# A windowed attention and gated convolution kernel: batch 0 in two token halves, rows of h turned by engine copies, loads not paced, new target times

## The chip, the cores and the metric

The kernel runs on one core of one Trainium2 chip. The metric is the device time of one execution in microseconds, the median of several runs. Before the change it is 241.77 us, the median of three runs (241.15, 241.77, 247.62).

A core has five engines that run side by side: TensorE (PE; its weight loads are shown apart, as PEld) for matmuls, VectorE (DVE), ScalarE (ACT) and GpSimd (POOL) for the rest of the arithmetic, and SyncE (SP), whose queue issues most DMAs here. Matmul results land in PSUM, eight banks of 2 KB on each of 128 partitions; all else lies in SBUF.

## What is computed

Attention in a window of 32 tokens to each side, for 8 batches, 8 heads, 576 tokens and 64 columns a head; its output, 512 columns a token, goes through a gated feed-forward block with a convolution of three tokens:

```python
scores = scale * np.matmul(q, k.transpose(0, 1, 3, 2))
mask = np.abs(pos[:, None] - pos[None, :]) <= 32
scores = np.where(mask, scores, -1000000000.0)
attn = np.exp(scores - max); attn = attn / sum(attn)
x = np.matmul(attn, v)                          # heads side by side: [8, 576, 512]
h = np.maximum(x @ w_in, 0.0)                   # [8, 576, 1024]
conv_out[t] = sum over k of conv_w[k] * hp[t + k]   # three tokens, zero outside
gate = 1.0 / (1.0 + np.exp(-conv_out))
out = h * gate @ w_out                          # [8, 576, 512], float32
```

## The kernel before

**The order.** The kernel first lists tasks, each with the engines that can do it (`kinds`, with a modelled duration), what it reads and writes, and a target time `t`. `Order.run` then walks a model of the machine: on each engine that comes free it takes, of the tasks that are ready, the one with the smallest target, finds free PSUM banks for it, and emits its instructions. Where a task has two engines it goes to the one that would be done first. The order of instructions on each engine is thus fixed when the kernel is built; on the chip each waits for what it needs. Targets come from the few numbers in `PARAMS` (line 832).

**Loads.** `loads(b)` (line 349) brings a batch: `q` and `k` as four DMAs of 576 KB, one for every four heads of each (all 128 partitions: 64 groups of nine tokens, two heads), and `v` as five blocks of 128 tokens (1024 runs of 256 bytes, fewer at the ends). There is one set of staging tiles (`qkst`, `vst`), which GpSimd casts to bf16 (`qkb`, `ve`); the next load of a tile waits for the cast. VectorE makes `vo`, the copy of `ve` that is shifted by 64 tokens. From batch 2 on, `paced()` makes each load wait for the landing of the load two before it:

```python
def paced():
    return before[-2:-1] if b > 1 and len(before) > 1 else []
```

`load_w_in` (2 x 1 MB) stands behind batch 0, `load_w_out` (seven DMAs, 2 MB) behind batch 1. Both go through the tile `ws`, which holds outputs later.

**Attention.** `transposes` turns `q` and `k` of four heads on TensorE, copies go to `qT`, `kT` on ScalarE or VectorE; `scores` makes the scores of a pair of heads in two parts of five and four token blocks, ScalarE takes the exponential, VectorE multiplies by the mask (one instruction per pair); `values` multiplies by `v`, with a column of ones that gives the sum; VectorE takes the reciprocal and writes `xn`; `x_turned` turns `xn` into `xT`.

**Feed-forward.** Two batches are cut into three chunks of 384 tokens (`ffn`, chunks 0 to 11). Chunk 1 crosses from one batch into the next and is done in two parts. `first` makes eight blocks of 128 rows of `h` in `hT`, with a relu. `gates` makes the convolution as 32x32 matmuls, which write rows of block `m` turned by 32 x (m mod 4) partitions, so that four matmuls run side by side. The product with the gate needs `h` turned alike: `moves` (line 688) does this by DMAs on SP's queue from `hT` to `gT`, two DMAs for each of three turns, for both halves of the blocks at once or (chunks 4, 7, 10 and 11) for each half:

```python
for lo, to, cnt in turn(s_):
    if len(qds) > 1:
        sync.dma_start(gate(m, to, to + cnt, 2, 4), taps(m, 1, lo, lo + cnt, 2))
```

ScalarE takes the tanh (the sigmoid is written with it), VectorE multiplies (`product`), `second` multiplies by `w_out` in three groups of 128 tokens, ScalarE copies out of PSUM, and a DMA stores.

Of the kernel before, what the change touches and what calls it, by code (L numbers as in the profile page):

```python
# [31 lines left out]
class Order:  # L32
# [3 lines left out]
    def __init__(self):  # L36
        self.tasks, self.writer, self.readers = [], {}, {}

    def add(self, kinds, emit, t, reads=(), writes=(), opens=None, ps=(), after=(), claims=()):


        deps = set(after)
# [10 lines left out]
        task = Task(len(self.tasks), kinds, emit, t, deps, opens, ps)  # L53
        task.soft = soft - deps
        for k in reads:
            self.readers.setdefault(k, []).append(task)
# [8 lines left out]
    def run(self, emit=True):  # L65
        free = {"PE": 0.0, "ACT": 2800.0, "DVE": 6000.0, "POOL": 4400.0, "SP": 800.0}
# [128 lines left out]
def kernel(  # L195
# [53 lines left out]
    hT_pp = [sb([128, MB, CH + (4 if i == 1 else 2)], BF16, f"hT{i}") for i in range(3)]  # L249
# [98 lines left out]

    def loads(b):
        i = b % NLD  # L350

        def load_qk(y, j):
# [4 lines left out]
            )  # L357

# [21 lines left out]
        if b < 2:  # L380
            x, dx = (-100.0 if b == 0 else -50.0), 0.1
        else:
            x, dx = t0 - PARAMS["LD"], Q["LX"]
# [3 lines left out]
        def paced():  # L387
            return before[-2:-1] if b > 1 and len(before) > 1 else []

        for j in range(NPH):  # L390
            for y in range(2):
                t = x + n * dx
                o.add({"SP": dma(256, 110)}, lambda e, y=y, j=j: load_qk(y, j), t,
                      writes=[("st", y, j)], after=paced())
                before.append(o.tasks[-1])
                o.add({"POOL": pl(1152)}, lambda e, y=y, j=j: cast_qk(y, j, e), t,
                      reads=[("st", y, j)], writes=[("b", i, y, j)])
                n += 1
        for c in range(NBLK):
            t = x + n * dx  # L400
            o.add({"SP": dma(1024, 21)}, lambda e, c=c: load_v(c), t, writes=[("vst", c)], after=paced())
            before.append(o.tasks[-1])
            o.add({"POOL": pl(512)}, lambda e, c=c: cast_v(c, e), t,
                  reads=[("vst", c)], writes=[("ve", i, c)])
            n += 1
        for cs in ((0, 2), (2, 4)) if b == 0 else ((0, 4),):
            for half in range(2):
                o.add({"DVE": dve(520 * (cs[1] - cs[0]), 4)},
                      lambda e, cs=cs, half=half: shift(half, cs), x + n * dx,
                      reads=[("ve", i, c + half) for c in range(*cs)],  # L410
                      writes=[("vo", i, c, half) for c in range(*cs)])

    def load_w_in():
        for h in range(2):
# [9 lines left out]
            o.add({"SP": dma(512, 95)}, load, -60.0, writes=[("ws", 4 * h + c) for c in range(4)])  # L424
            for c in range(KC):
                o.add({"POOL": pl(512)}, lambda e, h=h, c=c: cast(e, h, c), -60.0 + h,
                      reads=[("ws", 4 * h + c)], writes=[("w_in", h, c)])

    def load_w_out():
        rows = moe_w_out.rearrange("(h c p) f -> p h c f", c=4, p=128)  # L430
        for c in range(4):
            def load(e, c=c):
                for lo, at, n in turn(c):
# [5 lines left out]
            o.add({"SP": dma(256, 95, len(turn(c)))}, load, -40.0,  # L439
                  writes=[("ws", 4 * h + c) for h in range(2)])  # L440
            for h in range(2):
                o.add({"POOL": pl(512)}, lambda e, h=h, c=c: copy(e, w_out_sb[:, 4 * h + c, :], ws[:, 4 * h + c, :]),
# [18 lines left out]
    def conv_weights():  # L461
        ps = Banks(1)
        o.add({"PE": pe(200.0, "f32")},
              lambda e: tensor.matmul(bank(ps, 0)[:, 0:3 * MB], conv_w24, ident24, start=True, stop=True),
              5.0, opens=ps, writes=[("cw24",)])
        o.add({"DVE": dve(24)}, lambda e: vector.tensor_copy(
            out=conv_w_sb.rearrange("p k m -> p (k m)"), in_=bank(ps, 0)[:, 0:3 * MB]),
            5.0, reads=[("cw24",)], writes=[("cw",)], ps=[ps])
        o.add({"DVE": dve(768)}, lambda e: vector.tensor_tensor(
# [5 lines left out]
    def transposes(g2):  # L475
# [3 lines left out]
        i, n = b % NLD, g2 % NKT  # L479
        for y in range(2):  # L480
# [16 lines left out]
            o.add({"PE": pe(280.0, "rows")}, mm, t + Q["TR"],  # L497
# [311 lines left out]
    for b in range(B):  # L809
# [4 lines left out]
        if b == 1:  # L814
            load_w_out()
# [52 lines left out]
```

## Time and profile before

| | |
|---|---|
| median of three runs | 241.77 us |
| profiled execution, time of its own | 243.37 us |
| its span, first to last instruction | 241.7 us |
| mean granted TensorE clock | 0.972 |
| busy in the span: PE / DVE / ACT / POOL | 208.1 / 160.1 / 164.0 / 80.9 us |
| moved by DMA | 49.62 MB, 205 GB/s |

The profile is of one execution. All instructions bear line 274, that of a helper through which every instruction is issued, so groups are told apart by the tiles that they write and read (`hT<-pst` is the relu, `gT<-hT` a row move). An engine's busy time is the union of its instructions; that of TensorE holds the pipeline's ends, so 100% busy isn't its peak. In a timeline row stand the start and the duration in us, engine, line, operation, tile written and tiles read, and in brackets the idle time before it and what ended it; SPq is SP's queue as it issues DMAs.

### The profile page before, as it was taken

The numbers are of one execution on the slowest core, as the hardware profiler recorded it, in microseconds if no ns is written. First come the engines' busy times: TensorE is split into PE (matmuls) and PEld (weight loads), VectorE is DVE, ScalarE is ACT, GpSimd is POOL, SyncE is SP. The second block draws the span as 40 slices with busy tenths as digits, with TensorE's granted clock in tenths as the row PEclk, the third lists the DMA queues.
The fourth block names the chain that finished last, engine by engine and source line by source line (L and its number), as shares of the span: only waits on it lengthen the run. The fifth ranks groups of instructions, "written<-read, shape, count | busy, mean of one in ns | idle before, by whom it ended". The sixth has DMA issues, their size and how long they took to land. (4 is left out here: it accounts for less than half of the span.)

```text
span 241.7 us, 9128 instructions
## 1 busy us (share of the span) xinstructions
PE 208.1 (86%) x3878; PEld 124.3 (51%) x3906; DVE 160.1 (66%) x268; ACT 164.0 (68%) x291; POOL 80.9 (33%) x96
## 2 busy tenths in 40 slices
PE   1536995589998869999999998999999999999993
PEld 0425464365655454565455654655555655555541
DVE  7586166998575899546399779698684595524140
ACT  1650586445698576679977886679778885876751
POOL 5757744536613444662236517321000000000000
PEclk9999999758999997999999999999999999999999
DMA  6999999989698899969489989756132223342534
GB/s 237 292 289 392 248 233 223 275 229 337 168 290 186 217 293 355 328 186 278 98 207 356 264 225 281 161 129 205 37 129 55 79 105 68 123 110 54 177 113 181
DMA packets 67228, 49.62 MB, mean 205 GB/s; under 512 B 46172, under 2 KB 52340, under 8 KB 67188
## 3 DMA queue, kind: packets, MB, share of 16 engines
q1 hardware_dynamic: 67152, 49.03, 71.6%
q8 instruction: 30, 0.49, 0.9%
q14 instruction: 10, 0.08, 0.1%
q10 hardware_dynamic: 36, 0.01, 0.0%
HBM read 32.52 MB, written 9.44 MB: 174 GB/s over the span
## 5 line engine op out<-in xcount | busy, mean ns | idle before, releaser
L274 PE MATMUL pst<-xT,w_in_sb 128*128 128x385 bf16 (+2 forms) x416 | 75.4, 322 | 1.6 <-ACT xT L274 0.6
L274 PE MATMUL pst<-w_out_sb,gT 128*128 128x512 bf16 x260 | 64.3, 384 | 3.2 <-issue 2.2
L274 PEld LDWEIGHTS <-w_in_sb 128*128 128x128 bf16 x416 | 37.6, 100 | 25.8 <-issue 3.4
L274 ACT ACTIVATE hT<-pst 128x385 bf16<-128x385 f32 (+2 forms) x80 | 38.6, 489 | 11.1 <-PE pst L274 10.1
L274 DVE SCALAR_TENSOR_TENSOR gT<-tn,gT 128x384 bf16<-128x384 f32 (+2 forms) x52 | 42.4, 842 | 3.9 <-DMA gT<-hT 3.9
L274 POOL CAST ve<-vst 128x512 bf16<-128x512 f32 x40 | 29.4, 741 | 45.7 <-DMA vst<-in_v_dram 43.5
L274 ACT ACTIVATE attn<-pst 128x640 bf16<-128x640 f32 x64 | 39.4, 667 | 4.9 <-PE pst L274 4.9
L274 PEld LDWEIGHTS <-gT 128*128 128x128 bf16 x288 | 26.6, 99 | 31.0 <-issue 3.3
L274 ACT ACTIVATE tn<-pst 128x768 f32<-128x768 f32 (+1 forms) x52 | 37.4, 768 | 6.5 <-PE pst L274 4.6
L274 ACT COPY wst<-pst 128x512 f32<-128x512 f32 x36 | 21.2, 588 | 29.6 <-PE pst L274 28.1
L274 DVE TENSOR_TENSOR attn<-attn,mask 128x1152 bf16<-128x1152 bf16 x32 | 26.9, 846 | 12.3 <-ACT attn L274 12.1
L274 DVE TENSOR_TENSOR xn<-pst,rec 128x640 bf16<-128x640 f32 x32 | 25.8, 818 | 0.5
L274 DVE SCALAR_TENSOR_TENSOR gT<-tn,hT 128x384 bf16<-128x384 f32 (+1 forms) x26 | 14.7, 564 | 16.5 <-ACT tn L274 16.4
L274 POOL CAST qb<-qst 128x1152 bf16<-128x1152 f32 x16 | 19.9, 1242 | 16.2 <-DMA qst<-in_q_dram 12.5
L274 POOL CAST kb<-kst 128x1152 bf16<-128x1152 f32 x16 | 19.9, 1243 | 16.0 <-DMA kst<-in_k_dram 14.3
L274 PE MATMUL pst<-hT,diag_w 32*32 32x384 bf16 (+1 forms) x1248 | 21.2, 322 | 1.8 <-DVE xn L274 1.0
L274 ACT COPY xT<-pst 128x1024 bf16<-128x1024 bf16 (+1 forms) x16 | 11.8, 781 | 13.9 <-PE pst L274 13.9
L274 PEld LDWEIGHTS <-attn 128*64 128x64 bf16 x640 | 14.1, 119 | 13.6 <-issue 8.6
L274 PE MATMUL pst<-ve,attn 128*64 128x65 bf16 x384 | 17.4, 206 | 3.8 <-DVE attn L274 2.3
L274 PE MATMUL pst<-qT,kT 64*128 64x64 bf16 x576 | 17.5, 197 | 3.1 <-DVE kT L274 0.8
L274 PE MATMUL pst<-vo,attn 128*64 128x65 bf16 x256 | 15.6, 206 | 3.3 <-DVE vo L274 3.3
L274 PEld LDWEIGHTS <-kT 64*128 64x128 bf16 x576 | 12.2, 98 | 12.0 <-issue 9.2
(37 smaller groups left out, 163.4 us busy)
## 6 DMA issues: line engine op xcount, KB each, us to landing
qst<-in_q_dram SPq DMA_DIRECT2D x16, 576.0 KB, 6.4
kst<-in_k_dram SPq DMA_DIRECT2D x16, 576.0 KB, 7.3
out_dram<-wst SPq DMA_DIRECT2D x11, 768.0 KB, 5.8
vst<-in_v_dram SPq DMA_DIRECT2D x24, 256.0 KB, 5.5
vst<-in_v_dram SPq DMA_DIRECT2D x16, 192.0 KB, 5.9
wst<-in_moe_w_in_dram SPq DMA_DIRECT2D x2, 1024.0 KB, 7.9
gT<-hT SPq DMA_DIRECT2D x14, 144.0 KB, 3.6
gT<-hT SPq DMA_DIRECT2D x34, 48.0 KB, 2.1
```

Of the source, the lines that this page charges most:

```text
L274: return lambda *args, **kwargs: fixed(do(*args, **kwargs))
```

## The change

- **Batch 0 in halves.** `q` and `k` of batch 0 come as 16 DMAs of 144 KB on 64 partitions each (32 groups of nine tokens, two heads), the first half of the tokens of both before the second, with three blocks of `v` and half of `w_in` behind half 0 and the rest behind half 1. The first half's `k` is issued from ScalarE's queue. Casts, transposes, scores (four and five blocks), masks, values, reciprocals and products of batch 0 are made for each half, chunk 0's `first` too. A list `lead` holds the loads of batches 0 and 1, `w_in` and `w_out` to the order in which they are listed.
- **Rows turned by copies.** `moves` makes ten copies on VectorE or ScalarE (32 partitions each for turns by 32 and 96, 64 for the turn by 64) in place of six DMAs. `hT` begins one element later in its rows, so that the copies' source begins on four bytes.
- **Loads not paced.** `paced()` returns nothing.
- **New targets.** `PARAMS` is replaced, and a table `NUDGE` adds to the target of each kind of task a number for each batch or chunk. The casts of `w_in` may go to ScalarE too.

```diff
+        index = self.index + 20 * sub
+        t += self.nudge.get(name, {}).get(index, 0.0)
...
+        if line:
+            soft.add(line[-1])
...
-    hT_pp = [sb([128, MB, CH + (4 if i == 1 else 2)], BF16, f"hT{i}") for i in range(3)]
+    hT_pp = [sb([128, MB, CH + (6 if i == 1 else 4)], BF16, f"hT{i}")[:, :, 1:] for i in range(3)]
...
+        def load_half(y, j, half):
+            for e_ in range(2):
+                src = (q, k)[y][b, 4 * j + 2 * e_:4 * j + 2 * e_ + 2, 32 * RP * half:32 * RP * half + 32 * RP, :]
+                (scalar if y and not half else sync).dma_start(
+                    qkst[y][j][64 * e_:64 * e_ + 64, half, :, :].rearrange("p j d -> p (j d)"),
+                    bass.AP(src.tensor, src.offset, [[RP * D, 32], [S * D, 2], [1, RP * D]]),
+                )
...
         def paced():
-            return before[-2:-1] if b > 1 and len(before) > 1 else []
+            return []
...
+        if b == 0:
+            for half in range(2):
+                t = x + 3.0 * half
+                for j in range(NPH):
+                    for y in range(2):
+                        o.add("qk", {"SP": dma(128, 110, 0 if y and not half else 2)}, lambda e, y=y, j=j, half=half: load_half(y, j, half),
+                              t, writes=[("st0", y, j, half)], sub=half, line=lead)
+                        o.add("qc", {"POOL": pl(576)}, lambda e, y=y, j=j, half=half: cast_half(y, j, half, e), t,
+                              reads=[("st0", y, j, half)], writes=[("b0", y, j, half)], sub=half)
+                        t += 0.1
+                for c in (range(0, 3), range(3, NBLK))[half]:
+                    v_block(c, t)
+                    t += 0.1
+                v_shift((2 * half, 2 * half + 2), t)
+                load_w_in(half, t + 1.0)
+            return
...
+    def transposes_half(g2, y, half, t):
...
+            for x in range(RP):
+                for h in range(2):
+                    rows = slice(64 * h, 64 * h + 64)
+                    tensor.transpose(turned()[rows, x, :], half_of(y, j, half)[rows, x, :], ident[rows, rows])
...
-        for part, ts in enumerate((range(0, 5), range(5, 9))):
+        for part, ts in enumerate((range(0, 4), range(4, 9)) if first_ else (range(0, 5), range(5, 9))):
...
         for s_ in range(1, 4):
             ms = [4 * qd + s_ for qd in qds]
-
-            def move(e, m=ms[0], s_=s_):
-                for lo, to, cnt in turn(s_):
+            wide = 64 if s_ == 2 else 32
+            for lo in range(0, 128, wide):
+                to = (lo + 32 * s_) % 128
+
+                def move(e, m=ms[0], lo=lo, to=to, wide=wide):
                     if len(qds) > 1:
-                        sync.dma_start(gate(m, to, to + cnt, 2, 4), taps(m, 1, lo, lo + cnt, 2))
+                        copy(e, gate(m, to, to + wide, 2, 4), taps(m, 1, lo, lo + wide, 2))
                     else:
-                        sync.dma_start(gate(m, to, to + cnt), taps(m, 1, lo, lo + cnt))
...
+                o.add("mv", {"DVE": dve(n * len(qds) + 60, 3.4), "ACT": act(n * len(qds))},
...
+        if c == 0:
+            for m in range(MB):
+                first(c, m, 0, T0 + Q["A0"] + m * 0.5)
...
-PARAMS = {"P": 23.98, "T0": 17.65, "T1": 35.65, "T2": 7.73, "B1": 27.27, "LD": 15, "LEAD": 0,
...
+PARAMS = {"P": 26.5, "T0": 10, "T1": 34.66, "T2": 16, "B1": 22.98, "LD": 21.05, "LEAD": 6.54,
...
+NUDGE = {
+    "qk": {0: 72.02, 1: -5.05, 2: -18.01, 3: -48.45, 4: 22.78, 5: 87.66, 6: -20.9, 7: 1.68,
+        20: 9.36},
...
```

More of the change, by code (lines that the diff above doesn't have):

```diff
@@ L65, in run @@
     def run(self, emit=True):
-        free = {"PE": 0.0, "ACT": 2800.0, "DVE": 6000.0, "POOL": 4400.0, "SP": 800.0}
+        free = {"PE": 0.0, "ACT": 5400.0, "DVE": 6000.0, "POOL": 4400.0, "SP": 800.0}
         mode, channel, backlog = None, 0.0, []
@@ L346 @@
         start[c] = T1 + PARAMS["T2"] + (c - 2) * PC
+    lead = []
     def loads(b):
@@ L422, in cast @@
                 copy(e, w_in_sb[:, c, 512 * h:512 * h + 512], ws[:, 4 * h + c, :])
[L424 removed]
+            o.add("wi", {"SP": dma(512, 95)}, load, t, writes=[("ws", 4 * h + c) for c in range(4)], sub=h, line=lead)
             for c in range(KC):
[L426 to L427 removed]
+                o.add("wic", {"POOL": pl(512), "ACT": act(512)}, lambda e, h=h, c=c: cast(e, h, c), t,
+                      reads=[("ws", 4 * h + c)], writes=[("w_in", h, c)], sub=h)
     def load_w_out():
@@ L744, in product @@
                         scalar=1.0, in1=gate(m) if m0 else taps(m, 1), op0=ALU.add, op1=ALU.mult)
-            o.add({"DVE": dve(n * count)}, product, late,
+            o.add("pr", {"DVE": dve(n * count)}, product, late,
                   reads=[("tn", tn_i, u) for u in us] + ii,
-                  writes=[("g", c % 3, m + x, p_) for x in range(count) for p_ in halves])
+                  writes=[("g", c % 3, m + x, p_) for x in range(count) for p_ in halves],
+                  sub=qd + 2 * int(c == 1 and part == 0))
     tn_count = [0]
```

233 lines of the change are left out of this document (153 added, 80 removed), and 78 rows, old and new, of tables (NUDGE, PARAMS).

## The prediction

> **What bounds the kernel now.** I read the page's granted clock, then a table by stage, then the timelines of the first 55 us, then what the queue of loads does, last the groups by form. The stages (columns: TensorE, its weight loads, VectorE, ScalarE, GpSimd, each with its count; granted clock; DMA share; GB/s):
>
> ```profile
> core 0: us, PE busy (x) PEld busy (x) DVE busy (x) ACT busy (x) POOL busy (x), PEclk, DMA share, GB/s
> 0.00:25.50 25.50, 10.83 (x246) 8.83 (x246) 17.75 (x43) 9.57 (x15) 17.40 (x27) 1.00 1.01 307
> 25.50:54.50 29.00, 22.50 (x508) 15.53 (x508) 19.78 (x35) 16.67 (x29) 14.33 (x19) 0.84 0.95 236
> 54.50:100.00 45.50, 40.73 (x788) 24.63 (x778) 34.87 (x52) 33.01 (x62) 21.96 (x23) 0.95 0.94 268
> 100.00:165.00 65.00, 62.52 (x1231) 36.19 (x1234) 48.58 (x75) 51.13 (x92) 26.36 (x28) 1.00 0.82 222
> 165.00:220.00 55.00, 53.94 (x960) 30.56 (x969) 33.21 (x56) 42.79 (x77) 0.82 (x1) 1.00 0.31 96
> 220.00:242.00 22.00, 17.61 (x175) 8.57 (x176) 5.95 (x10) 10.87 (x19) 0.00 (x0) 1.00 0.40 138
> ```
>
> There are two kernels in one. From 100 us on TensorE is busy 134.1 of 142 us at full clock, so only less matmul waiting could help there. Before 54.5 us it is busy 33.3 of 54.5 us, with the DMA share at 0.95 to 1.01: the start waits for bytes. Between the two lies a stage with 4.8 us of TensorE idle and a clock of 0.95, some 2 us more. What the start waits for, from the timelines of TensorE, GpSimd and the loads' queue (start, duration, what):
>
> ```profile
> 4.76 1.14 POOL L274 CAST qb<-qst 128x1152 bf16<-128x1152 f32 x1 [1.65 <-DMA qst<-in_q_dram]
> 10.15 1.15 POOL L274 CAST kb<-kst 128x1152 bf16<-128x1152 f32 x1 [0.78 <-DMA kst<-in_k_dram]
> 16.49 0.99 POOL L274 CAST ve<-vst 128x512 bf16<-128x512 f32 x1 [0.56 <-DMA vst<-in_v_dram]
> 21.63 2.29 POOL L274 CAST w_in_sb<-wst 128x512 bf16<-128x512 f32 x4 [0.44 <-DMA wst<-in_moe_w_in_dram]
> 25.54 4.12 PE L274 MATMUL pst<-xT,w_in_sb 128*128 128x385 bf16 x16 [0.55 <-ACT xT L274]
> 28.58 1.15 POOL L274 CAST kb<-kst 128x1152 bf16<-128x1152 f32 x1 [0.81 <-DMA kst<-in_k_dram]
> 34.57 0.62 POOL L274 CAST ve<-vst 128x512 bf16<-128x512 f32 x1 [1.53 <-DMA vst<-in_v_dram]
> 39.22 0.21 PE L274 MATMUL pst<-ident,kb 64*128 64x64 bf16 x2 [2.17 <-issue]
> 40.23 1.03 DVE L274 COPY vo<-ve 64x2080 bf16<-64x2080 bf16 x1
> 42.11 3.27 POOL L274 CAST w_out_sb<-wst 128x512 bf16<-128x512 f32 x4 [1.39 <-DMA wst<-in_moe_w_out_dram]
> 54.62 2.37 PE L274 MATMUL pst<-w_out_sb,gT 128*128 128x512 bf16 x7
> 31.72 2.81 PE L274 MATMUL pst<-xT,w_in_sb 128*128 128x385 bf16 x20
> 36.38 0.44 PE L274 MATMUL pst<-ident,qb 64*128 64x64 bf16 x18
> 5.07 1.28 ACT L274 ACT_TABLE_LOAD   x1 [5.07 <-DVE conv_w_sb L274]
> 0.80 0.44 SPq L274 DMA_DIRECT2D qst<-in_q_dram  x1
> 30.07 4.13 SPq L274 DMA_DIRECT2D wst<-in_moe_w_out_dram  x7
> 34.58 8.04 SPq L274 DMA_DIRECT2D gT<-hT  x6
> 42.72 0.55 SPq L274 DMA_DIRECT2D qst<-in_q_dram  x1
> ```
>
> Batch 0 is whole at about 16.3 us, `w_in` at 21.6, batch 1 at 34.5, `w_out` near 43. Yet the first `w_in` matmul comes at 25.5 and the first `w_out` matmul at 54.6. Batch 1's `v` is there at 34.5, but its shift to odd blocks starts at 40.2. SP's queue is held 8 us by six row moves, which wait for relus, so batch 2's first load issues at 42.7.
>
> **The change, part by part.** Durations are of the profiled execution, 243.37 us with a span of 241.7, so 1.7 us lie around the span. The median of the three runs is 241.77, that is 1.6 us below the profiled execution; I sum against 243.4 and take the 1.6 off at the end.
>
> (a) *Batch 0 in two token halves.* The bytes are the same, only their order differs. From the casts above, batch 0's `q` and `k` (2.36 MB) land from 0.8 to about 10 us, the five blocks of `v` (1.18 MB) from there to 16.3, `w_in` (2.1 MB) to 21.6. In the new order (half 0 of `q`,`k`; three `v` blocks; half of `w_in`; the rest alike) these rates give: half 0 of `q`,`k` at 6, `v` 0 to 2 at 10, `w_in` half 0 at 12.6, half 1 of `q`,`k` at 16, all `v` at 18.5, `w_in` half 1 at 21. Attention of half 0 then ends near 17 us. Matmuls of blocks 0 to 3 over 193 columns can run at once, but that is a fourth of the 5.2 us that the chunk needs (32 matmuls at 0.14 to 0.26 us, by 2.81/20 and 4.12/16; I take 0.16). Blocks 4 to 7 wait for 21 plus a cast, half 1 of attention ends near 24.5. At 25.5 us the new kernel is therefore 2.6 to 3 us of matmuls ahead, not 8: gain 3 us. If the transfers keep no rate the gain is nil; if half 0's work all fits below 21 us it is 5.
>
> Its price: 16 loads of 144 KB in place of 4 of 576, at 0.44 us of issue each. Four go by ScalarE's queue, which has no work then (its first is at 5.07 us, a table load), the others by SP while the DMA share is already 1. If that cover were gone, 12 x 0.44 = 5.3 us of issue would stand before `w_in`. Twice the `q`,`k` transposes of batch 0 (72 more, 0.4 us for 18) and a few more masks, reciprocals and products (0.2 to 0.8 us) run in a stage where TensorE idles 15 us and VectorE 8: nothing. The chunk's relus double in number (8 more of 0.35 us, at half the columns): nothing, in the same gap.
>
> (b) *Moves off SP.* 102 DMAs go. Their groups, and the rows that the copies are nearest to:
>
> ```profile
> gT<-hT SPq DMA_DIRECT2D x14, 144.0 KB, 3.6
> gT<-hT SPq DMA_DIRECT2D x14, 96.0 KB, 3.4
> gT<-hT SPq DMA_DIRECT2D x34, 48.0 KB, 2.1
> L274 SPq DMA_DIRECT2D gT<-hT x102: 496/627/1922, 34.6 to 230.2; - x102
> DVE gT L274 <- DMA gT<-hT: 3.9, 2, 2.1
> L274 DVE TENSOR_TENSOR attn<-attn,mask 128x1152 bf16<-128x1152 bf16 x32 | 26.9, 846 | 12.3 <-ACT attn L274 12.1
> L274 DVE TENSOR_TENSOR xn<-pst,rec 128x640 bf16<-128x640 f32 x32 | 25.8, 818 | 0.5
> L274 DVE RECIPROCAL rec<-pst 128x10 f32<-128x10 f32 x32 | 6.5, 211 | 11.8 <-PE pst L274 10.0 <-ACT hT L274 1.4
> L274 DVE COPY vo<-ve x18: 425/698/1587, 13.8 to 167.2; 64x2080 bf16<-64x2080 bf16 x14, 64x1040 bf16<-64x1040 bf16 x4
> L274 DVE COPY vo<-ve 64x2080 bf16<-64x2080 bf16 x14 | 12.4, 884 | 0.5
> L274 ACT COPY qT<-pst 128x576 bf16<-128x576 bf16 x23 | 14.2, 647 | 0.3 <-PE pst L274 0.3
> L274 ACT COPY xT<-pst 128x1024 bf16<-128x1024 bf16 x10 | 10.1, 1017 | 13.7 <-PE pst L274 13.7
> ```
>
> The moves themselves cost VectorE only 3.9 us of waiting in all; what they cost is SP's order. With SP free, batch 2's loads can issue once `w_out` is under way, and nothing paces them. With batch 1 whole at the same 34 us, but no moves between it and VectorE, its attention should end near 44 instead of 52 us: four pairs, each about 2.5 us of VectorE (mask, reciprocal, product, a share of the copies). I take the first `w_out` matmul at 46.5 instead of 54.6, 8 us earlier, the 3 us of (a) in it. Bounds: 2 us (only (a)'s lead, less what the order loses) and 11 us (attention right behind the last byte). In 54.5 to 100 us earlier loads of batches 2 and 3 win back half of the 4.8 + 2 us lost: 3 us, bounds 0 and 6.
>
> (c) *170 copies.* Seven chunks take ten copies of 768 columns; chunk 1 (two parts) and chunks 4, 7, 10, 11 take twenty of 384: 70 + 100. The two lengths of `vo` give 0.26 ns a column undisturbed ((698 - 425)/1040), so 0.35 us for 768 and 0.25 for 384; the `vo` mean of 884 against 698 says that 0.19 us of waiting comes on top while GpSimd casts (until 165 us). ScalarE, by its 576 and 1024 rows, needs 0.81 and 0.49 us. All on VectorE: 25 + 25 = 50 us, with the waiting on the two thirds before 165 us about 70; all on ScalarE 105.
>
> Where would they lie? A chunk takes some 17 us (ten chunks from 64 to 235). From 100 to 165 us that is 3.8 chunks, 54 copies, 26 us with the waiting. VectorE and ScalarE together have 16.4 + 13.9 = 30.3 us free there: it fits, barely. From 54.5 to 100 us 38 copies, 18 us, against 23 free. From 165 on 46 copies, 14 us, against 34 free. So the copies are hidden as a sum, but at 90% and more of two engines that free TensorE's banks some matmuls will wait. I take +3 us, bounds 0 and +17 (below). A copy before a product waits for a relu where a DMA was waited for: behind it on VectorE stand masks and products, for which TensorE waits.
>
> The Trainium skill speaks against this part: SBUF — State Buffer, section "Who interferes with whom", says that VectorE in a two-port copy mode and GpSimd take one port pair as a lock, so that whichever starts second is blocked for the whole instruction of the other. The trace agrees in kind (0.19 us a copy on average, 1.59 at most); by the rule a copy could wait up to a `q` cast, 1.15 us here.
>
> (d) *New targets* only reorder; they are in the choices above.
>
> Sum: 243.4 - 8 - 3 + 3 = 235.4, less 1.6: **233.8, say 234 us**.
>
> **Rivals.** (1) *The copies make VectorE the bound until 165 us* (slower). If the order, which knows nothing of the waiting, leaves nearly all on VectorE, 92 copies x 0.48 = 44 us meet 10.6 + 16.4 = 27 us of free VectorE in 54.5 to 165: 17 us over. With the start's gain, and no more: 243.4 - 8 - 3 + 17 = 249.4, median 248. It decides once VectorE passes 95% there. For: VectorE was on the last chain at 141 to 150 us even now. Against: ScalarE may take copies and relus. Chance 0.18.
>
> (2) *The halves load at half rate.* Loads of 64 partitions may not use what 128 do: moves of 64 partitions (96 KB) took 3.4 us, those of 96 partitions (144 KB) 3.6. If 2.36 MB at 307 GB/s took twice 7.7 us, all that follows, `w_out` too, comes 7.7 us later and the 8 us are gone: 243.4 - 0.3 - 3 + 3 = 243.1, median 241.5. Against: both partition halves stand next to each other in the queue. The Trainium skill, SBUF — State Buffer, section "Can I just issue two DMAs to hit both halves?", says that they serialize, which would be this rival. Chance 0.12.
>
> (3) *The lead is given back.* An earlier start meets the same stage of thin loads at 54.5 to 100 us (the unpaced loads wait for casts that free their buffers), or TensorE's waits grow later: half of (b) is lost, 239.5 and median 238. Chance 0.12.
>
> **How the numbers follow.** Forecast 0.58, by itself 227 to 238. Range 225 to 248: (1) at its top, the gains of (a) to (c) at their better bounds, less what can't all come together, at its foot (243.4 - 11 - 6 - 1.6 = 224.8). A measurement here tells about 2% from no change: below 236.9 faster, above 246.6 slower. Faster: 0.52 of the forecast and 0.06 of (3), 0.58. Slower: 0.14 of (1), 0.04 of (2), 0.18. Same: 0.24.
>
> **What would show it.** Right: first `w_in` matmul before 20 us, first `w_out` matmul at 45 to 48, TensorE over 95% busy from there, VectorE near 195 us busy in all, copies of 768 near 0.35 us after 165 us and 0.5 before. Wrong: VectorE over 95% in 100 to 165 with TensorE under 90% (rival 1); the last `w_in` cast after 25 us (rival 2); first `w_out` matmul at 47 but TensorE idle 5 us and more up to 100 (rival 3).

## The result and the profile after

The changed kernel takes 255.96 us, the median of four runs (252.6 to 257.04); the kernel before, in the same rounds, 241.67 us. The ratio is 1.0515 with a 95% interval of 1.038 to 1.0651; a second measurement of six runs, told below, gives 1.0655 [1.0607, 1.0703]. Ratios and intervals leave out runs more than 1.5% above the shortest of their kernel, while the medians take all. The forecast was 234 us. The change is slower by 12 to 16 us. The profiled execution took 257.04 us, 1.8% above the shortest of the four, at a granted clock of 0.944.

The table by stage, of the kernel after, with the columns of the prediction's table:

```profile
core 0: us, PE busy (x) PEld busy (x) DVE busy (x) ACT busy (x) POOL busy (x), PEclk, DMA share, GB/s
0.00:25.50 25.50, 12.55 (x275) 10.10 (x276) 12.28 (x42) 11.76 (x21) 12.78 (x25) 1.00 1.00 254
25.50:54.50 29.00, 19.45 (x475) 14.95 (x474) 24.01 (x44) 18.77 (x41) 19.08 (x22) 0.74 1.05 275
54.50:100.00 45.50, 37.61 (x755) 22.87 (x745) 43.04 (x77) 28.08 (x55) 20.63 (x22) 0.87 0.69 193
100.00:165.00 65.00, 59.88 (x1136) 34.30 (x1145) 62.80 (x114) 52.04 (x92) 23.30 (x24) 1.00 0.74 197
165.00:220.00 55.00, 53.49 (x986) 31.33 (x992) 46.64 (x93) 48.08 (x87) 2.86 (x5) 1.00 0.17 60
220.00:256.00 36.00, 30.46 (x379) 15.47 (x380) 20.98 (x50) 25.15 (x47) 0.00 (x0) 0.98 0.24 89
```

Multiply TensorE's busy time by the granted clock for a rough measure of the matmul work done in a stage (it ignores that a busy TensorE isn't at its peak). Up to 25.5 us the changed kernel is 12.55 - 10.83 = 1.7 us ahead. Then it falls behind: 14.4 against 18.9 in the second stage, 32.7 against 38.7 in the third, 59.9 against 62.5 in the fourth, 53.5 against 53.9 in the fifth. Together 13.5 us lost, 11.8 net, which is nearly the whole difference of the two spans (255.3 - 241.7 = 13.6). The loss lies between 25 and 165 us, and there VectorE is at 83%, 95% and 97%, against 68%, 77% and 75% before (82%, 95% and 96% in the profile of the second measurement). From 54.5 to 165 us VectorE is the bound, as the experiments below bear out. The 4.5 us of the second stage are another matter. From 25 to 35 us the granted clock is 0.66, where it was 1.00 before, and TensorE's 7.66 busy us make 5.1 us of work against 9.5: nearly the whole loss of the stage. The attention of half 1 runs there in short bursts of matmuls, which wait 0.3 to 0.8 us each for VectorE's masks and shifts of `v`. The kernel that leaves out both the copies and most of GpSimd's casts (below) loses as much there. The kernel after, busy times and the chain that ended last:

```profile
PE 213.4 (84%) x3985; PEld 129.0 (51%) x4010; DVE 209.8 (82%) x415; ACT 183.9 (72%) x338; POOL 78.7 (31%) x96
```

```profile
PE 41%; DVE 36%; ACT 14%; issue 5%; DMA 2%; SPq 1%; POOL 0%; DVEq 0%; ACTq 0%; POOLq 0%
```

In the kernel before, this line read "PE 40%; DVE 3%", but that chain reaches back to 129 us only, so the two can't be set side by side. Of the kernels below whose chains reach back to the start, those without the copies have VectorE at 10% and 14%, the one without the casts at 11%, and the one without both at 5%. What happens where the start's lead is lost, from the timelines of the kernel after (start, duration, what):

```profile
8.78 0.67 POOL L283 CAST qb<-qst 128x576 bf16<-128x576 f32 x1 [1.68 <-DMA qst<-in_q_dram]
19.08 2.75 PE L283 MATMUL pst<-xT,w_in_sb 128*128 128x193 bf16 x16
24.53 1.45 POOL L283 CAST w_in_sb<-wst 128x512 bf16<-128x512 f32 x2 [2.01 <-DMA wst<-in_moe_w_in_dram]
38.13 0.40 SPq L283 DMA_DIRECT2D qst<-in_q_dram  x1
47.78 0.54 PE L283 MATMUL pst<-hT,diag_w 32*32 32x384 bf16 x12 [3.10 <-issue]
49.90 1.47 DVE L283 SCALAR_TENSOR_TENSOR gT<-tn,hT 128x384 bf16<-128x384 f32 x1
51.30 2.36 DVE L283 SCALAR_TENSOR_TENSOR gT<-tn,gT 128x384 bf16<-128x384 f32 x2
54.62 3.10 POOL L283 CAST ve<-vst 128x512 bf16<-128x512 f32 x3
55.13 0.61 PE L283 MATMUL pst<-w_out_sb,gT 128*128 128x512 bf16 x1 [0.49 <-DVE gT L283]
57.66 1.27 POOL L283 CAST qb<-qst 128x1152 bf16<-128x1152 f32 x1
57.84 2.70 DVE L283 SCALAR_TENSOR_TENSOR gT<-tn,gT 128x192 bf16<-128x192 f32 x2
60.47 4.11 DVE L283 TENSOR_TENSOR attn<-attn,mask 128x1152 bf16<-128x1152 bf16 x4
```

And one window with the columns of the table by stage, of the kernel after and then of the kernel before:

```profile
50.00:60.00 10.00, 5.82 (x111) 2.09 (x111) 10.00 (x9) 3.93 (x8) 9.17 (x8) 0.50 1.05 297
50.00:60.00 10.00, 9.89 (x181) 6.38 (x182) 9.19 (x15) 5.79 (x11) 5.21 (x5) 0.72 0.99 305
```

From 50 to 60 us VectorE is busy without a gap and yet gets only nine instructions done, where it did 15. A product of 384 columns takes 1.47 us there, a pair of 192 columns 2.70 us. Beside them GpSimd casts for 9.17 of the 10 us (5.21 before). TensorE is busy for 5.82 us at a granted clock of 0.50, where it was 9.89 us at 0.72.

### The profile page after: what moved, and what is told of

It is laid out like the page before. It is cut to its first block, busy times and chain, and to the rows that moved or that the text cites. A ratio compares the mean times of both kernels' runs of the same rounds, so it can differ in the third digit from the quotient of the medians.

```text
span 255.3 us, 9229 instructions
## 1 busy us (share of the span) xinstructions
PE 213.4 (84%) x3985; PEld 129.0 (51%) x4010; DVE 209.8 (82%) x415; ACT 183.9 (72%) x338; POOL 78.7 (31%) x96
## 4 chain that ended last, share of the span: by engine, by line
PE 41%; DVE 36%; ACT 14%; issue 5%; DMA 2%; SPq 1%; POOL 0%; DVEq 0%; ACTq 0%; POOLq 0%
PE pst L283 41%; DVE gT L283 18%; DVE attn L283 5%; ACT tn L283 4%; DVE xn L283 4%; ACT hT L283 4%; ACT gT L283 3%; DMA qst<-in_q_dram 2%; DVE vo L283 2%; DVE qT L283 2%; DVE xT L283 2%; ACT attn L283 1%; DVE kT L283 1%; DVE hT L283 1%; SPq L283 1%
## 5 line engine op out<-in xcount | busy, mean ns | idle before, releaser
L283 PE MATMUL pst<-xT,w_in_sb 128*128 128x385 bf16 (+3 forms) x448 | 73.9, 314 | 2.2 <-DVE hT L283 0.9
L283 DVE COPY gT<-hT 32x384 bf16<-32x384 bf16 (+3 forms) x130 | 46.5, 358 | 4.7 <-ACT hT L283 2.3
L283 ACT ACTIVATE hT<-pst 128x385 bf16<-128x385 f32 (+3 forms) x92 | 40.0, 456 | 10.7 <-PE pst L283 10.0
L283 ACT ACTIVATE attn<-pst 128x640 bf16<-128x640 f32 (+1 forms) x64 | 38.4, 656 | 3.2 <-PE pst L283 3.0
L283 DVE TENSOR_TENSOR attn<-attn,mask 128x1152 bf16<-128x1152 bf16 (+2 forms) x36 | 28.6, 809 | 8.5 <-ACT attn L283 8.3
L283 POOL CAST qb<-qst 128x1152 bf16<-128x1152 f32 (+1 forms) x18 | 20.2, 1122 | 32.6 <-DMA qst<-in_q_dram 25.8
L283 ACT COPY gT<-hT 32x384 bf16<-32x384 bf16 (+3 forms) x40 | 25.1, 628 | 2.6 <-DVE hT L283 1.7
L283 DVE TENSOR_TENSOR xn<-pst,rec 128x640 bf16<-128x640 f32 (+2 forms) x36 | 25.9, 740 | 0.5
L283 POOL CAST kb<-kst 128x1152 bf16<-128x1152 f32 (+1 forms) x18 | 21.3, 1186 | 12.8 <-DMA kst<-in_k_dram 10.2
L283 PEld LDWEIGHTS <-diag_w 32*32 32x32 bf16 x1248 | 12.5, 88 | 20.0 <-issue 17.3
L283 PEld LDWEIGHTS <-attn 128*64 128x64 bf16 x640 | 14.4, 120 | 14.8 <-DVE attn L283 7.5
```

What stands on the lines that cost most here:

```text
L283: return lambda *args, **kwargs: fixed(do(*args, **kwargs))
```

## The experiments

I held three theories. C: the copies and what they wait for (VectorE and GpSimd hold each other up) cost the time. S: the start, halves and unpaced loads, costs instead of gaining. T: the targets suit the kernel's own model of the machine and not the chip. A price below is a difference of medians, or of ratios times 241.7 us where the runs come from different rounds. Where "order kept" is said, each engine's instructions stand in the changed kernel's order, only those named are gone.

### One part alone in the kernel before

The copies alone: `moves` as after, `hT` one element later, all else as before.

```diff
...
-                        sync.dma_start(gate(m, to, to + cnt, 2, 4), taps(m, 1, lo, lo + cnt, 2))
+                        copy(e, gate(m, to, to + wide, 2, 4), taps(m, 1, lo, lo + wide, 2))
```

> The kernel before with the row copies alone (10 or 20 copies a chunk on VectorE or ScalarE, hT shifted by one element; batch 0 whole, loads paced, old targets). Theory C (the copies fill VectorE, which waits for GpSimd's casts on top): 250 to 256 us, VectorE over 95% busy between 60 and 165 us, the copies of 768 columns at 0.43 us or more. Theory S (the loss comes from the start and the loads: halves, no pacing): within 2% of before, 238 to 246 us. Theory T (targets that fit a model and not the chip): within 2% of before.

261.98 us, ratio 1.0789 [1.072, 1.0857]. The copies alone cost some 19 us, more than the 8 to 14 us of theory C. The run also takes the DMA moves away, and its order is made anew, so not all of this need be the copies' own work. Two rows of its table by stage, its busy times, and two of its copies by form (busy us, mean in ns, idle time before them):

```profile
54.50:100.00 45.50, 37.00 (x774) 23.14 (x772) 41.35 (x70) 31.97 (x60) 17.68 (x20) 0.88 0.85 232
100.00:165.00 65.00, 57.01 (x998) 32.70 (x1004) 60.12 (x101) 50.06 (x85) 24.52 (x26) 0.95 0.68 180
```

```profile
PE 213.3 (82%) x3877; PEld 125.3 (48%) x3906; DVE 211.9 (81%) x393; ACT 192.5 (74%) x336; POOL 80.9 (31%) x96
```

```profile
L274 DVE COPY gT<-hT 32x768 bf16<-32x768 bf16 x34 | 16.4, 483 | 0.9
L274 ACT COPY gT<-hT 32x768 bf16<-32x768 bf16 x22 | 18.2, 829 | 1.3 <-DVE hT L274 0.8
```

VectorE is at 91% and 92% in the two stages (theory C had over 95%), and TensorE 3.7 and 5.5 us below the kernel before. From 165 to 220 us, with only 3.35 us of casts beside them, the copies cost little: TensorE is busy 53.1 of 55 us there, 53.9 before. The theory of a middle that VectorE bounds holds with the copies alone.

The loads not paced, alone:

```diff
-            return before[-2:-1] if b > 1 and len(before) > 1 else []
+            return []
```

> The kernel before with the loads not paced, nothing else. Theory C: within 2% (238 to 245 us), since the loads are not what binds. Theory S: 245 us or more, with GpSimd's casts and the DMA share bunched between 40 and 65 us. Theory T: within 2%.

247.48 us, 1.0161 [1.0073, 1.0248]: no gain, rather a loss of 2 to 6 us. With the old targets SP's queue lets batch 2 in at 43.7 us all the same, because the row moves still stand in it.

The halves of batch 0, alone, with the held order of the first loads:

```diff
+        if b == 0:
+            for half in range(2):
+                ...
+                        o.add("qk", {"SP": dma(128, 110, 0 if y and not half else 2)}, lambda e, y=y, j=j, half=half: load_half(y, j, half),
```

> Batch 0 in two token halves with DMA moves, paced loads and the old targets (the new load order, and the casts of w_in allowed on ScalarE, come along). Theory C: 236 to 243 us, a first w_in matmul near 19 us and a small gain. Theory S: 245 us or more, since the loads of 64 partitions are slow (178 GB/s in the first 10 us of the changed kernel against 274) and all later loads come 2.5 us later. Theory T: within 2%.

247.58 us (244.12 to 248.0), against 242.6 for the kernel before in the same rounds (no interval for this one). The first stage and the last cast of `w_in` on GpSimd, of this kernel:

```profile
0.00:25.50 25.50, 13.51 (x274) 10.29 (x274) 12.64 (x43) 11.06 (x18) 12.48 (x24) 1.00 1.01 248
```

```profile
25.23 1.49 POOL L283 CAST w_in_sb<-wst 128x512 bf16<-128x512 f32 x2 [1.86 <-DMA wst<-in_moe_w_in_dram]
```

In the same 25.5 us 248 GB/s were moved instead of 307, at a full DMA share: the bytes came later, not only in another order. This holds throughout: the six kernels here with whole loads moved 293 to 307 GB/s in this stage, the 13 profiles with halves of 144 KB 244 to 264. The lead of 2.7 us of matmuls is there, and the rest is late. The cost is some 5 us by the medians and 1.5 us by the shortest run.

### The changed kernel with one part taken back

Row moves by DMA again, the order made anew:

```diff
-                        copy(e, gate(m, to, to + wide, 2, 4), taps(m, 1, lo, lo + wide, 2))
+                        sync.dma_start(gate(m, to, to + cnt, 2, 4), taps(m, 1, lo, lo + cnt, 2))
```

> The changed kernel with its rows moved by DMA as before; halves, unpaced loads and new targets stay (the moves have no nudge). Theory C: 238 to 245 us, most of the loss is gone. Theory S: 250 to 256 us, since the first 95 us stay as they are. Theory T: 250 us or more, since the targets were made for other work.

253.57 us, 1.0431 [1.0357, 1.0504]: VectorE is at 160.0 us as in the kernel before, but the time isn't. DMAs make 21% of the chain that ended last and SP's queue 8%, so the targets, which were found for copies, seem to order moves badly; no run shows this by itself. So this run doesn't price the copies. That needs the order kept:

```diff
-                        copy(e, gate(m, to, to + wide, 2, 4), taps(m, 1, lo, lo + wide, 2))
+                        pass
...
```

> The changed kernel with its order of instructions kept and the 170 row copies left out (the products read h as it stands in hT, unturned). Theory C (the copies' time on VectorE and ScalarE is the loss): 234 to 242 us, VectorE near 165 us busy. Theory S (start and loads): 250 us or more, since the first 95 us and the loads stay. Theory T (the order itself fits the chip badly): 246 us or more.

248.07 us, 1.0236 [1.0193, 1.0279]. Its busy times:

```profile
PE 210.8 (86%) x3985; PEld 128.3 (52%) x4010; DVE 164.8 (67%) x285; ACT 162.1 (66%) x298; POOL 78.4 (32%) x96
```

VectorE's busy time is the 165 us that theory C had, but its 234 to 242 us aren't met; the last experiment takes this up. Nor do the copies make the stretch from 50 to 60 us. VectorE is as full without them:

```profile
50.00:60.00 10.00, 5.79 (x118) 2.15 (x113) 10.00 (x10) 4.42 (x9) 8.65 (x8) 0.50 0.92 253
```

Then the other side of the contention, GpSimd's 54 casts of `q`, `k` and `v` from batch 2 on, left out with the copies in place. (There are nine a batch: GpSimd's instructions fall from 96 to 42. The expectations count 78, and 13 and 65 further down; the profiles show 54, 9 and 45.) The edit also frees the attention of these batches from waiting for its loads, as does the control behind it:

```diff
...
-            copy(e, ve_pp[i][:, c, :, 0:64], vst[:, c, :, :])
+            if b < 2:
+                copy(e, ve_pp[i][:, c, :, 0:64], vst[:, c, :, :])
```

> The changed kernel, order kept, with GpSimd's casts of q, k and v left out from batch 2 on (attention of those batches reads the bf16 tiles of batches 0 and 1). Theory C with the waiting for GpSimd as a main part: VectorE's copies of 768 columns fall from 0.43 to 0.36 us, its other groups too, and the time by 6 us or more, more than in the kernel before. Without it (the copies' own time alone binds): less than 3 us. Theory S: 4 us or more, since loads no longer wait for casts, with copies as slow as before.

243.82 us, 1.0049 [1.0001, 1.0097]. VectorE does the same 415 instructions, and by form the two-input products and masks shrink as the copies do (busy us, mean in ns):

```profile
PE 212.0 (86%) x3985; PEld 128.3 (52%) x4010; DVE 190.6 (77%) x415; ACT 183.5 (74%) x338; POOL 26.3 (11%) x42
```

```profile
L283 DVE SCALAR_TENSOR_TENSOR gT<-tn,gT 128x768 bf16<-128x768 f32 x22 | 20.9, 948 | 0.2
L283 DVE TENSOR_TENSOR attn<-attn,mask 128x1152 bf16<-128x1152 bf16 x28 | 20.5, 750 | 2.3 <-ACT attn L283 2.2
L283 DVE COPY gT<-hT 32x768 bf16<-32x768 bf16 x42 | 15.2, 361 | 0.9
L283 DVE TENSOR_TENSOR xn<-pst,rec 128x640 bf16<-128x640 f32 x28 | 22.5, 818 | 0.5
```

The same rows in the kernel after, with GpSimd's casts:

```profile
L283 DVE TENSOR_TENSOR attn<-attn,mask 128x1152 bf16<-128x1152 bf16 x28 | 23.8, 867 | 1.7 <-ACT attn L283 1.6
L283 DVE SCALAR_TENSOR_TENSOR gT<-tn,gT 128x768 bf16<-128x768 f32 x22 | 23.4, 1061 | 0.2
L283 DVE COPY gT<-hT 32x768 bf16<-32x768 bf16 x42 | 18.1, 431 | 0.8
L283 DVE TENSOR_TENSOR xn<-pst,rec 128x640 bf16<-128x640 f32 x28 | 22.5, 818 | 0.5
```

The last row, a product that reads its large input from PSUM, takes 818 ns with and without the casts. So 209.8 - 190.6 = 19.2 us of VectorE's busy time is waiting for GpSimd, and taking it away gives back 11 to 15 us of the time, by the two measurements of the changed kernel. Its control is the same edit in the kernel before:

> The kernel before, order kept, with the same casts left out: the control for the run above. Theory C: 0 to 3 us less than before, since VectorE has room there. Theory S: 2 to 4 us less.

241.47 us, 0.9945 [0.9905, 0.9986]. There too VectorE loses waiting:

```profile
PE 207.0 (87%) x3878; PEld 123.4 (52%) x3906; DVE 148.6 (63%) x268; ACT 163.9 (69%) x291; POOL 29.5 (12%) x42
```

160.1 - 148.6 = 11.5 us, but the time falls by some 1 us only: VectorE had room. The waiting was in the kernel all along, and nearly free.

The old targets in the changed kernel:

```diff
-PARAMS = {"P": 26.5, "T0": 10, "T1": 34.66, ...
+PARAMS = {"P": 23.98, "T0": 17.65, "T1": 35.65, ...
-NUDGE = { ...
+NUDGE = {}
```

> Halves, copies and unpaced loads with the old PARAMS and no nudges. The copies alone cost 20 us with the old targets. Theory C: 258 to 268 us, and what the new targets win is the difference from 256. Theory T: 250 us or less, the new targets lose.

267.36 us, 1.1063 [1.1008, 1.1118]. The new targets are the one part of the change that helps, by 10 to 13 us, in a kernel with copies.

### Loads, and both suspects at once

Each half of `q` and `k` by one transfer onto 128 partitions:

```diff
-                    qkst[y][j][64 * e_:64 * e_ + 64, half, :, :].rearrange("p j d -> p (j d)"),
-                    bass.AP(src.tensor, src.offset, [[RP * D, 32], [S * D, 2], [1, RP * D]]),
+                qkst[y][j][:, half, :, :].rearrange("p j d -> p (j d)"),
+                bass.AP(src.tensor, src.offset, [[RP * D, 32], [S * D, 4], [1, RP * D]]),
```

> The changed kernel with its order kept to the instruction, but each half of batch 0's q and k loaded by one transfer onto all 128 partitions (8 transfers of 288 KB) in place of two of 144 KB onto 64 partitions each. The rows of batch 0 land on other partitions than the kernel reads them by, so batch 0's output is of other rows; the work on every engine is the same. Theory S (the halves arrive at 178 GB/s in the first 10 us where the whole loads had 274, and the start is late by it): the first 10 us go back to 250 GB/s or more, the last w_in cast starts 2 to 3 us earlier than 25.9, and the time falls by 2 to 4 us, to about 252 to 254. Theory C (the copies and the casts that wait on each other set the time up to 165 us, the start is hidden behind them): the start comes earlier and the time stays at 255 to 257.

258.49 us, 1.0682 [1.0584, 1.078]: no faster. The first stage moved 276 GB/s instead of 254, below the 293 to 307 of whole loads, and its first 10 us 187 instead of 178, far from the 274 of the kernel before. GpSimd's last casts of `w_in`, which wait for the transfer, started at 24.3 us instead of 24.5. (The 25.9 us of the expectation is ScalarE's last cast, which waits for other work of ScalarE, and so is the 26.7 us of this run.) That a transfer has 64 partitions isn't what makes the halves late, at most a part of it.

Copies and casts left out together:

> The changed kernel, order kept, without the 170 row copies (the products read h unturned) and without GpSimd's casts of q, k and v from batch 2 on. Alone the copies' absence gave 8 us and the casts' absence 12 us. Theory C as contention (the copies cost time because VectorE and GpSimd wait for one another, so each saving is largely the same time): the two together give little more than the casts alone, 242 to 244. Rival, plain sums (the copies cost VectorE's own 40 us of work, the casts cost GpSimd's buffers and loads, and the two have nothing to do with each other): the savings add to 20 us, 235 to 237.

241.11 us, 0.9978 [0.9922, 1.0035]. Busy times and three stages of this kernel:

```profile
PE 211.6 (88%) x4010; PEld 127.3 (53%) x4010; DVE 152.2 (64%) x285; ACT 161.6 (68%) x298; POOL 26.1 (11%) x42
```

```profile
25.50:54.50 29.00, 19.95 (x472) 15.00 (x467) 17.25 (x34) 17.81 (x40) 13.99 (x19) 0.74 1.05 280
54.50:100.00 45.50, 44.12 (x935) 26.61 (x935) 34.51 (x65) 33.51 (x65) 0.00 (x0) 0.98 0.94 244
100.00:165.00 65.00, 64.47 (x1263) 37.03 (x1256) 47.43 (x79) 49.61 (x90) 0.00 (x0) 1.00 0.67 198
```

From 54.5 us on TensorE is at 97% and 99%: the middle is cured. The second stage isn't. Its work, 19.95 x 0.74 = 14.8 us, is that of the changed kernel (14.4), with VectorE at 59%. So neither the copies nor these casts cost the 4.5 us there; they came with the new start and order. In the third and fourth stage the changed kernel has 32.7 and 59.9 us of work; without the copies it is 35.0 and 63.4, without the casts 38.5 and 63.0, without both 43.2 and 64.5. And still this kernel is only level with the kernel before, and with the control (0.9945), so that the start and the new order by themselves won nothing. Adding the copies to it costs 0.7% (1.0049 - 0.9978), 2 us, which the intervals don't separate from nothing, though they are 38 us of VectorE's work (190.6 - 152.2); adding them beside the casts costs 8 us and more. Contention holds, the plain sum (235 to 237) falls.

Batch 0 whole again, and the loads paced again, each with the order made anew:

```diff
-        if b == 0:
+        if False:
...
-        v_shift((0, 4), x + n * dx)
+        for cs in ((0, 2), (2, 4)) if b == 0 else ((0, 4),):
+            v_shift(cs, x + n * dx)
+        if b == 0:
+            load_w_in(0, -60.0)
+            load_w_in(1, -59.0)
...
```

```diff
-            return []
+            return before[-2:-1] if b > 1 and len(before) > 1 else []
```

> The changed kernel with batch 0 loaded and worked whole, as before the change; copies, unpaced loads and new targets stay, and the order is made anew (its own model ends it at 224.3 us, as it does the changed kernel). Theory S (the halves cost at the start: alone they made 241.7 into 247.6): 250 to 253. Theory T (the new targets were found for the halves, so without them the order is worse, and the halves pay in that order): 256 or more.

> The changed kernel with the loads paced again as before the change (each load after that of two v blocks before it); the rest stays, and the order is made anew (its own model ends it at 230.9 us, against 224.3). Theory T (the model orders the kernels rightly and only its level is off): 262. Theory S (unpaced loads of batches 1 and 2 fall together with the copies at 50 to 60 us, where VectorE was busy for all 10 us and TensorE for 5.8, and the model doesn't see it): 256 or less, and VectorE busy for less than 9 of the 10 us from 50 to 60.

254.04 us, 1.052 [1.044, 1.0599], and 259.73 us, 1.0769 [1.0685, 1.0853]. In both VectorE is still busy for all of 50 to 60 us. Taking back the halves wins 2 to 3 us by the medians; the intervals separate this from nothing only for the second measurement of the changed kernel. Pacing isn't what was missing: with it this kernel is no faster.

### Which casts, and what the rest is worth

Only batch 2's nine casts left out (`if b != 2`), then only the 45 of the batches after it (`if b < 3`):

> The changed kernel, order kept, without GpSimd's 13 casts of batch 2 alone (they run at 48 to 67 us, beside the stretch in which VectorE is busy for all of 10 us and TensorE for 5.8; batch 2 is then computed from the bfloat16 rows of batch 0). All 78 casts from batch 2 on were worth 12.1 us. Theory B (the bunch: the unpaced loads bring batch 2's casts against the first products of gT and the first copies, where everything behind waits): these 13 casts carry most of it, 245 to 250 us. Theory E (evenly spread: each cast that VectorE meets costs its share, about 0.16 us): 13 of 78 carry 2 us, 253 to 255.

> The counterpart: order kept, batch 2's 13 casts run, the 65 of batches 3 to 7 are left out. Theory B: 250 to 254, VectorE still busy for all of 50 to 60 us. Theory E: 65 of 78 carry 10 us, 245 to 247. If the two parts add up, this time and the one without batch 2's casts lie together 12 us below twice 255.96.

252.51 us, 1.036 [1.0287, 1.0434], and 246.77 us, 1.0127 [1.002, 1.0235]. Against 255.96 that is 3.5 and 9.2 us, against 12.1 for all: the parts add up. Against the second measurement, by the ratios, it is 7 and 13 us, against 15 for all, so that they overlap. Per cast it is 0.4 to 0.8 us in batch 2 and 0.2 to 0.3 us after. The bunch from 48 us on costs at least some twice its share, but most of the price is spread.

New targets without copies, found by a search over the same order model (`PARAMS` as before, another `NUDGE`), with batch 0 whole and in halves, loads paced:

> The kernel before (batch 0 whole, rows moved by DMA, loads paced) with new targets alone, found by a search over the same order model: its end goes from 235.2 us with the old targets in this form (w_in's casts shared by GpSimd and ScalarE) to 229.8; the kernel before itself stands at 232.0 there. Theory T (the model misses VectorE's waiting and the loads, but kernels with DMA moves all run 10 to 18 us above it, kernels with copies 26 to 33, so that within a family a better order is a faster kernel): 239 to 242, level with the kernel before or up to 1% faster. Rival (the model's order says nothing at this size): 245 to 250, as the other kernels with DMA moves and one edit.

> The kernel before with batch 0 in halves, DMA moves and paced loads, and new targets found for this form in the same way (model: 230.0 us, 232.8 with the old targets). With the old ones it took 247.6. Theory S (the halves' late loads cost whatever the order): 245 to 248. Theory T (the halves lacked an order made for them): 240 to 243.

244.21 us, 1.008 [1.0037, 1.0123], and 249.75 us, 1.0224 [1.0129, 1.0319]. Neither beats the kernel before, though the model ends them 2 us earlier. With targets of their own the halves cost 5.5 us by the medians and 3.5 us by the ratios. No version here that does all of the work is faster than the kernel before.

Last, the changed kernel and the one without copies in the same rounds:

> The changed kernel itself, beside the one without copies on the same chip, to narrow the interval that all prices hang on (1.038 to 1.065 so far). If the copies and GpSimd's casts share a price (contention), the ratio stays at 1.045 to 1.06, so that the copies cost 2% and more beside the casts, where they cost 0.7% without them. If it is 1.035 or less, the copies cost about 1% with or without casts, and the shared price was only scatter.

> The changed kernel, order kept, without the 170 row copies (the products read h unturned), in the same rounds. Both theories: 1.02 to 1.028 as before; what decides is its distance to the changed kernel, 2% and more for contention, about 1% for none.

257.03 us (256.52 to 258.01), 1.0655 [1.0607, 1.0703], and 247.45 us as the median of twelve, which spread from 238.98 to 250.46 us. Of these and the four earlier ones, 4 took 238.98 to 242.98 us and 12 took 246.32 to 250.46 us. The median of the 4 is 241.5 us, level with the 241.7 of the kernel before; the two shortest by themselves give the ratio 0.9929 [0.9868, 0.9989]. So the copies cost 8 to 10 us by the medians, and 15 to 17 us against the four lowest; with no casts beside them, 2 to 3 us. The rule that I wrote down, 2% or more, is met either way. It also corrects a reading from the first four runs, that the casts cost 6 to 7 us even without copies (1.0236 against 0.9978): the four lowest are level with the kernel that has neither (241.5 against 241.1 us). So the copies alone cost 2 to 3 us, the casts alone 0 to 7, and the two together 13 to 16 us against the kernel with neither. What is more than the sum is the contention.

## Why the prediction was wrong

**The copies, part (c): the term that failed.** The durations were right: 352 ns after 165 us for 768 columns where 0.35 us was worked out, 252 for 384 where 0.25 was, 829 and 507 ns on ScalarE for 0.81 and 0.49. The waiting was there too, 454 ns before 165 us: 0.10 us a copy, half of the 0.19 assumed. (The "1.59 at most" of the prediction is the longest copy of `vo` as a whole, and not a wait.) The kernel after, VectorE by form, from 45 to 165 us and then from 165 us on:

```profile
L283 DVE COPY gT<-hT 32x768 bf16<-32x768 bf16 x28 | 12.7, 454 | 0.6
L283 DVE SCALAR_TENSOR_TENSOR gT<-tn,hT 128x384 bf16<-128x384 f32 x11 | 8.4, 762 | 0.6 <-ACT tn L283 0.4
...
L283 DVE SCALAR_TENSOR_TENSOR gT<-tn,hT 128x384 bf16<-128x384 f32 x12 | 6.6, 554 | 2.6 <-ACT tn L283 2.4
L283 DVE COPY gT<-hT 32x768 bf16<-32x768 bf16 x10 | 3.5, 352 | 0.2
```

What failed is the step from there to +3 us. I put the waiting on the new copies alone, 0.19 us each. It falls on VectorE's products and masks too, wherever they read SBUF and meet a cast: the product of 384 columns takes 762 ns before 165 us and 554 after, and the whole goes from 11.5 us of waiting in the kernel before to 19.2. VectorE came to 209.8 us busy, where 195 was said. And I took the free time of two engines as room for the copies, when 130 of the 170 went to VectorE; the order, which prices no waiting, saw nothing wrong. "It fits, barely" was true of the sum (62.8 of 65 us) and no reason to expect 3 us: with VectorE at 95% and 97%, TensorE's work fell by 6.0 and 2.6 us. The price was 8 to 17 us beside the casts. With the 11 us of gains below that didn't come, this accounts for the way from 234 us to 256: 234 + 11 + 5 to 14.

The Trainium skill, SBUF — State Buffer, section "Who interferes with whom", states more than I used: besides the two-port copies it names VectorE instructions with two inputs in SBUF as contending with GpSimd's reads. The rows above agree, with 554 against 762 ns. I had read the first rule and weighed it for the copies only.

**Rival 1** named the mechanism: nearly all copies on VectorE, over 95% in 100 to 165 us (it was 97%, with 130 of the 170 copies on VectorE in all), the price there up to 17 us. Its second mark, TensorE under 90%, wasn't met (92%). Its time, 248 us, was too low by about the 11 us of gains that it kept.

**The start, parts (a) and (b).** The first `w_in` matmul came at 19.08 us, before 20 as said, and the lead was 1.7 us in the place of 2.6 to 3. It was lost again by 35 us, while the second half's attention ran at a granted clock of 0.66. And half 0 of `q` and `k` was whole at 8.8 us and not at 6, and `w_in` at 24.5 and not at 21: I had let the loads keep the rate that they had whole, and the halves had 254 GB/s for 307. That is rival 2's effect; its cause, transfers of 64 partitions, isn't confirmed, since the wide halves were no faster. What slows them stays open. The first `w_out` matmul came at 55.1 us, not 46.5. Batch 2's first load did issue earlier, at 38.1 us for 42.7, and this is what I had counted on. But GpSimd's first cast of batch 2 began at 48.3 us, and at 47.9 before; behind it the casts came closer, 9.2 us of them from 50 to 60 us for 5.2, beside VectorE's first products of the gate. The new order also puts batch 1's four masks behind these products. The last of them in the kernel before, all four in the kernel after, and all four with neither copies nor casts:

```profile
47.08 0.70 DVE L274 TENSOR_TENSOR attn<-attn,mask 128x1152 bf16<-128x1152 bf16 x1
60.47 4.11 DVE L283 TENSOR_TENSOR attn<-attn,mask 128x1152 bf16<-128x1152 bf16 x4
53.09 2.76 DVE L283 TENSOR_TENSOR attn<-attn,mask 128x1152 bf16<-128x1152 bf16 x4
```

So the step of (b) that failed is the end of batch 1's attention "near 44". Batch 1 was whole at 37 us and not at 34 (GpSimd's last cast of its `v` began at 37.25 us), and with the moves gone the new targets, said to "only reorder", put products ahead of its masks, which the waiting then made longer. The 8 us of (b) and the 3 us of the stage behind it were nil; without copies and casts the kernel is level with the one before. The price of the halves, "nothing", was wrong too: alone they cost some 5 us by the medians.

**The targets, part (d)**, which I left at nothing, win 10 to 13 us in a kernel with copies, so that without them the forecast would have been further off; other new ones, found for DMA moves, won nothing. The kernel's own model, in which they were found, ends the changed kernel at 224.3 us and the one before at 232.0. Against the medians that is 31.7 and 9.8 us too early. The other kernels with copies whose end in the model is on record run 29 to 33 us above it, those with DMA moves 10 to 20. The gain that the model saw is smaller than the waiting that it leaves out.

What is open: why the halves load slower; why the runs of the kernel without copies spread from 239 to 250 us; how the loss from 25 to 35 us divides between the halves and the new order; and the 3.1 us in which TensorE waits for nothing that the profile shows ahead of the convolution at 47.8 us (2.1 to 4.0 us in the kernels with the same order).

## What to carry to other kernels

Waiting that costs nearly nothing on an engine with room becomes the price when work is moved onto that engine: take the waiting of all its instructions, not of the new ones, and measure it by leaving out the other party. An engine's free time in a stage, taken as a sum, says little when the work would fill it: from 100 to 165 us TensorE lost 2.6 and 5.5 us of busy time with VectorE at 97% and 92%, and none at 88%, without the casts. A planner that leaves out a contention can fill the very engine that suffers from it. And look whether a stage's loss stays when the suspects are left out: here that of the second stage did.

## What the runs showed of the hardware that was not expected

GpSimd's casts stretch VectorE's instructions with two inputs in SBUF as well as copies: 762 ns beside casts against 554 without for a product of 384 columns, 431 against 361 ns on average for a copy of 768, 867 against 750 ns for a mask. A product that reads its large input from PSUM isn't stretched: 818 ns both times. Left out from batch 2 on, they free 11.5 us of VectorE's busy time in the kernel before, 12.6 in the changed one without copies (164.8 to 152.2) and 19.2 in the changed one.

In the first 25.5 us the same DMA share (1.00 and 1.01) moved 254 GB/s in halves and 307 whole.
